# Grouping an attention pair's TensorE calls by array form, and queueing weight splits one tile later

## The chip, the cores and the metric

The kernel runs on one core of a Trainium2 chip. The metric is the device time of one execution in microseconds (us), from a few runs; the span of a profiled execution runs from the first to the last instruction. In the profile PE is TensorE's matmuls, PEld its weight loads, ACT ScalarE, DVE VectorE, POOL GpSimd, and SP the queue that issues the DMAs.

## The reference

Three blocks follow each other. Tokens are 1792 (4 batches of 448), the model width is 768, 12 heads of 64.

```python
scores = scale * np.matmul(q, k.transpose(0, 1, 3, 2)) - np.log(S)
attn = 1.0 / (1.0 + np.exp(-scores))
x = np.matmul(attn, v)                      # heads side by side: 1792 x 768
rms = np.sqrt(np.mean(x * x, axis=-1, keepdims=True) + 1e-06)
xn = x / rms * rms_g
g = xn @ w_gate; val = xn @ w_val           # 768 -> 1536
x = g * sigmoid(g) * val @ w_out            # 1536 -> 768
a = x @ w1; b = x @ w2                      # 768 -> 1024
out = (a * b @ w3) @ w_out2                 # 1024 -> 1024 -> 768
```

q, k and v are float32, and the weights arrive as float64. w3 and w_out2 can be multiplied with each other first; the kernel does that.

## The kernel before, in words

Everything is unrolled, and a list scheduler in the framework fixes the order of the instructions on each engine from the order in which the code issues them; tile pools set which buffer must come free before an instruction may write. Each engine works its own list strictly in turn.

**Weights.** A weight tile (128 rows of 768 or 512 columns) is loaded as pairs of 32-bit words into a `wd` buffer (two of these, `load_double`, L86), turned into float32 by `to_float` (L89 to L110: one Abs on ACT, L94, then four DVE operations, L95, L96, L104, L107, into a `wf` buffer, of which there are two), and split into a high and a low fp32r part by `split_weight`: a copy on ACT (L113) and a subtraction on POOL (L114). The results are `ws` tiles, of which there are four; `o` tiles are the same for w_out2. `Weights.split_to` (L174) does decode and split of a tile in one go. Every product of weights and activations then takes three matmuls (L230 to L232, or L266 to L268 for w3 by w_out2) of 128 x 128 on 448 or 384 columns.

**Attention.** A pair of heads is one step, 24 pairs in all. `load_pair` brings q, k and v of the pair into one `raw` tile. `scores(p, c)` multiplies key block c with q into a PSUM tile `sc` (two of these) and ACT takes the sigmoid into an `a` tile (L304). Blocks 0 to 2 use the array as two halves of 64 rows, one head in each (L300); block 3 holds the last 64 keys of both heads and uses the whole array (L303). `attend(p, c)` multiplies v with `a` into the PSUM tile `av` (one of these): blocks 0 to 2 as two halves of 64 columns (L317), block 3 on the whole array (L319). So there are three forms of the array: 64 x 128, 128 x 64 and 128 x 128, and the weight products use the last. After block 3 the result goes out: ACT copies it (L322), squares it (L327, L330), POOL adds the squares (L331), and a DMA writes it to memory (L324).

**Stages.** The first is the loop over `i` (L543): pairs 0 to 11, the eight decodes of w_out2 (`decode_wo2`, two in each of the first four passes), and, from i = 5 on, 16 groups of w3 by w_out2 (`w3o_group`, 24 matmuls each, two in a pass). It ends with `rms_norm(1)`; x tiles of batch 0 (`split_x`, L357 load, L358, L245, L246) are made in its last six passes. The second stage (about 200 to 650 us) is a list of units (`first_units`): accumulations of 18 or 36 matmuls for the gate, value, out, w1 and w2 products of batches 0 and 1. Between the units the steps of the other 12 pairs are dealt out evenly, six to a pair:

```python
yield lambda: scores(p, 0)
yield lambda: scores(p, 1)
yield lambda: (attend(p, 0), scores(p, 2))
yield lambda: (attend(p, 1), scores(p, 3))
yield lambda: attend(p, 2)
yield lambda: (attend(p, 3), load_pair(p + 2))
```

`run` (L527) loads ahead, runs a unit, and splits the next weight tile. The third stage (650 us on) has no attention: Winograd products of batches 2 and 3.

## Time and profile before

| | |
|---|---|
| runs | 1145.35, 1145.58, 1146.7 us, median 1145.58 us |
| profiled execution | 1145.92 us, span 1144.2 us |
| PE busy | 1112.4 us, 97% of the span |
| DVE, ACT, POOL busy | 632.3, 474.4 and 373.6 us |
| mean granted TensorE clock | 0.994 of full speed |

In the rows further down, a line of the timeline gives start, length, engine, line of the code, operation, tile written and read, shapes, how many records it merges (a call in one of the half forms leaves four records, a whole-array call of attention two), and in brackets how long the engine stood idle before and what it waited for. A PE length contains pipeline time, so the step from one start to the next is the better measure. The table by stage gives for each stretch the busy time of every engine, the granted clock (1.00 is 2.4 GHz, half is 1.2 GHz), the DMA engines' share and GB/s.

### The profile page before, as it was taken

To read this page: it belongs to the slowest core of one execution; us is meant where nothing else is said; L and a number is where in the kernel's file an instruction comes from. 1 tells how busy PE (TensorE), PEld (TensorE's weight loads), DVE (VectorE), ACT (ScalarE), POOL (GpSimd) and SP (SyncE) were. 2 spreads that over 40 slices of the span, in tenths; PEclk is the share of its full clock that TensorE was granted. 3 is DMA by queue.
4 is the path that set the end of the run, shared out by engine and by line. 5 is a ranking of instruction groups with operands and counts; after the bars stand their busy time and mean duration, and the time that the engine had idled before them with its cause. 6 is when DMAs were issued, how large, how long until landed. Compare 5 with 4: busy or idle time off the path is not lost.

```text
span 1144.2 us, 13902 instructions
## 1 busy us (share of the span) xinstructions
PE 1112.4 (97%) x5204; PEld 898.4 (79%) x5204; DVE 632.3 (55%) x873; ACT 474.4 (41%) x768; POOL 373.6 (33%) x276
## 2 busy tenths in 40 slices
PE   7689998999999999999999999999999999999998
PEld 2256767778777877877777799999989999899997
DVE  4765347764546554543544255598998222777600
ACT  6655554444434433433443334444444232433321
POOL 2431223122222312121222222466666222566420
PEclk9989998999999999999999999999999999999999
DMA  6655556553535354444443225221112210111131
GB/s 245 225 162 174 186 183 228 173 198 120 173 111 200 117 178 140 165 147 147 166 142 142 68 79 163 100 74 56 56 56 71 69 56 19 56 58 54 37 100 52
DMA packets 54930, 141.41 MB, mean 124 GB/s; under 512 B 5200, under 2 KB 28752, under 8 KB 54864
## 3 DMA queue, kind: packets, MB, share of 16 engines
q1 hardware_dynamic: 54864, 140.53, 36.6%
q8 instruction: 41, 0.67, 0.2%
q14 instruction: 25, 0.20, 0.1%
HBM read 105.91 MB, written 34.60 MB: 123 GB/s over the span
## 4 chain that ended last, share of the span: by engine, by line
PE 80%; DVE 2%; DMA 1%; POOL 0%; ACT 0%; issue 0%; SPq 0%; POOLq 0%; ACTq 0%
PE psm L230 18%; PE psm L231 17%; PE psm L232 17%; PE w L230 7%; PE w L231 7%; PE w L232 7%; PE sc L300 3%; PE av L317 3%; PE sc L303 1%; PE av L319 1%; DMA xs<-x 1%; POOL ws L114 0%; DVE s L438 0%; DVE wd L147 0%; DVE s L145 0%
## 5 line engine op out<-in xcount | busy, mean ns | idle before, releaser
L114 POOL TENSOR_TENSOR ws<-wf,ws 128x768 fp32r<-128x768 f32 (+1 forms) x104 | 175.5, 1687 | 546.8 <-ACT ws L113 546.8
L230 PE MATMUL w<-w,ws 128*128 128x448 f32 x420 | 154.4, 368 | 2.0 <-ACT w L245 1.5
L231 PE MATMUL w<-w,ws 128*128 128x448 f32 x420 | 154.3, 367 | 0.0
L232 PE MATMUL w<-w,ws 128*128 128x448 f32 x420 | 154.0, 367 | 0.0
L94 ACT ACTIVATE mag<-wd 128x768 f32<-128x768 f32 (+1 forms) x76 | 65.4, 860 | 158.3 <-DVE wf L96 60.0
L96 DVE TENSOR_SCALAR wf<-mag 128x768 uint32<-128x768 uint32 (+1 forms) x76 | 44.0, 580 | 139.8 <-POOL ws L114 138.1
L230 PE MATMUL psm<-x,ws 128*128 128x448 f32 x288 | 112.5, 391 | 1.7 <-ACT x L245 1.7
L231 PE MATMUL psm<-x,ws 128*128 128x448 f32 x288 | 106.7, 370 | 3.0 <-DVE x L246 3.0
L113 ACT ACTIVATE ws<-wf 128x768 fp32r<-128x768 f32 (+1 forms) x104 | 78.9, 759 | 72.6 <-PE psm L232 39.8
L114 POOL TENSOR_TENSOR ws<-wd,ws 128x384 fp32r<-128x384 f32 x80 | 87.7, 1112 | 61.1 <-ACT ws L113 61.1
L230 PE MATMUL psm<-hm,ws 128*128 128x448 f32 x288 | 107.4, 373 | 0.0
L232 PE MATMUL psm<-x,ws 128*128 128x448 f32 x288 | 106.2, 369 | 0.0
L231 PE MATMUL psm<-hm,ws 128*128 128x448 f32 x288 | 105.7, 367 | 0.0
L232 PE MATMUL psm<-hm,ws 128*128 128x448 f32 x288 | 104.9, 364 | 0.0
L304 ACT ACTIVATE a<-sc,bias_s 128x896 f32<-128x896 f32 x96 | 86.1, 907 | 25.3 <-PE sc L300 16.7
L114 POOL TENSOR_TENSOR ws<-s,ws 128x384 fp32r<-128x384 f32 x60 | 71.8, 1200 | 63.2 <-ACT ws L113 56.1
L95 DVE TENSOR_SCALAR mag<-mag 128x768 f32<-128x768 f32 (+1 forms) x76 | 43.8, 577 | 83.6 <-ACT mag L94 83.3
L107 DVE SCALAR_TENSOR_TENSOR wf<-wd,wf 128x768 uint32<-128x768 uint32 (+1 forms) x76 | 87.1, 1146 | 1.4
L230 PEld LDWEIGHTS w<-w,ws 128*128 128x128 f32 x420 | 78.7, 188 | 11.1 <-ACT w L245 1.8
L300 PE MATMUL sc<-raw 64*128 64x448 f32 x288 | 74.1, 596 | 11.1 <-ACT a L304 5.7
L232 PEld LDWEIGHTS w<-w,ws 128*128 128x128 f32 x420 | 78.9, 188 | 7.4
L231 PEld LDWEIGHTS w<-w,ws 128*128 128x128 f32 x420 | 78.8, 188 | 7.2
(117 smaller groups left out, 2161.0 us busy)
## 6 DMA issues: line engine op xcount, KB each, us to landing
raw<-in_qkv SPq DMA_DIRECT2D x24, 736.0 KB, 6.1
wd<-in_wo SPq DMA_DIRECT2D x20, 768.0 KB, 4.9
wd<-in_w SPq DMA_DIRECT2D x16, 768.0 KB, 4.9
wd<-in_wg SPq DMA_DIRECT2D x12, 768.0 KB, 4.7
wd<-in_wv SPq DMA_DIRECT2D x12, 768.0 KB, 4.9
wd<-in_w SPq DMA_DIRECT2D x16, 512.0 KB, 4.1
w<-wf SPq DMA_DIRECT2D x16, 384.0 KB, 2.5
wf<-w3o SPq DMA_DIRECT2D x24, 256.0 KB, 2.8
```

The lines of the kernel that those rows point to most:

```text
L94: nc.scalar.activation(mag, hi.bitcast(F32), AF.Abs)
L95: nc.vector.tensor_scalar(out=mag, in0=mag, scalar1=HI_MIN, scalar2=HI_MAX, op0=ALU.max, op1=ALU.min)
L96: nc.vector.tensor_scalar(out=u, in0=mag.bitcast(U32), scalar1=3, scalar2=0x3FFFFFFF, op0=ALU.logical_shift_left, op1=ALU.bitwise_and,)
L107: nc.vector.scalar_tensor_tensor(out=u, in0=lo, scalar=29, in1=u, op0=ALU.logical_shift_right, op1=ALU.bitwise_or)
L113: nc.scalar.activation(t[:, 0, :w], f[:, :w], AF.Copy)
L114: nc.gpsimd.tensor_tensor(out=t[:, 1, :w], in0=f[:, :w], in1=t[:, 0, :w], op=ALU.subtract)
L230: nc.tensor.matmul(ps, wl, xt[:, 0, :], start=first, stop=False)
L231: nc.tensor.matmul(ps, wh, xt[:, 1, :], start=False, stop=False)
L232: nc.tensor.matmul(ps, wh, xt[:, 0, :], start=False, stop=last)
L300: nc.tensor.matmul(ps[:, j, :S], r[d, k], r[d, Q0 : Q0 + S], start=True, stop=True)
L304: nc.scalar.activation(a, ps[:, :, :S], AF.Sigmoid, bias=bias_s, scale=1.0 / math.sqrt(D))
L317: nc.tensor.matmul(ps[d, :], r[:, v + j * D : v + (j + 1) * D], a[:, j, :], start=(c == 0), stop=False)
```

## The change

Five edits. `attend` takes a list of blocks and begins the accumulation with block 3; what it did after the last block is now `take_out`. In the loop over `i`, a pair's attend calls run one pass later, all four in one row once the w3o groups run (i = 5 on), else as (3, 0) and (1, 2) between the score calls. In the second stage a pair is two steps, `first_half` (all of the pair before, then scores 0 and 1) and `second_half` (scores 2 and 3). `split_to` and `decode_wo2` now decode a tile first and then split the tile decoded before it (`late`, `finish`); `get` splits the tile at once if that has not happened. The first pair's `raw` tile is loaded by three DMAs, of 576, 384 and 512 columns, instead of one of 1472.

```diff
--- before.py
+++ after.py
@@ -120,6 +120,7 @@
 
         def __init__(self):
             self.seq, self.raw, self.split = [], {}, {}
+            self.late = None
             self.n_load = self.n_split = self.out = 0
             self.loaded, self.blocks = [], self.winograd_blocks()
 
@@ -171,30 +172,44 @@
                 self.raw[self.n_load] = t
                 self.n_load += 1
 
-        def split_to(self, n):
+        def split_to(self, n, flush=False):
+
             n = min(n, len(self.seq) - 1)
             while self.n_split <= n and len(self.split) < self.BUFS:
                 i = self.n_split
                 self.load_to(i)
                 src, kt, double, keep = self.seq[i]
                 f = self.raw.pop(i)
+                w = WT if kt is None else kt * P
+                if double:
+                    f = to_float(f, w)
+                    if keep is not None:
+                        nc.sync.dma_start(out=keep, in_=f[:, :w].rearrange("p (k c) -> p k c", c=P))
+                    self.out -= 1
+                self.finish()
                 t = wp.tile([P, 2, WT], F32R, tag="ws", bufs=self.BUFS, name="ws")
+                self.split[i] = [t, 2]
+                self.n_split += 1
                 if kt is None:
                     for j in range(2):
                         split_weight(t[:, :, j * WH : (j + 1) * WH], next(self.blocks), WH)
+                elif double:
+                    self.late = (i, t, f, w)
                 else:
-                    w = kt * P
-                    if double:
-                        f = to_float(f, w)
-                        if keep is not None:
-                            nc.sync.dma_start(out=keep, in_=f[:, :w].rearrange("p (k c) -> p k c", c=P))
                     split_weight(t, f, w)
                     self.out -= 1
-                self.split[i] = [t, 2]
-                self.n_split += 1
+            if flush:
+                self.finish()
+
+        def finish(self):
+            if self.late:
+                split_weight(*self.late[1:])
+                self.late = None
 
         def get(self, i):
             self.split_to(i)
+            if self.late and self.late[0] == i:
+                self.finish()
             t = self.split[i]
             t[1] -= 1
             if not t[1]:
@@ -250,8 +265,9 @@
 
     def decode_wo2(j):
         f = to_float(raw2.pop(j), DM)
+        W.finish()
         t = wo2p.tile([P, 2, DM], F32R, tag=f"o{j}", name=f"o{j}")
-        split_weight(t, f, DM)
+        W.late = (None, t, f, DM)
         o2.append(t)
 
     NH = DM // 2
@@ -286,7 +302,10 @@
     def load_pair(p):
         if p < NP:
             t = raw[p] = at([P, RAWW], F32, "raw")
-            nc.sync.dma_start(out=t, in_=qkv[p // HP, p % HP])
+
+            cuts = (0, S + P, V0, RAWW) if p == 0 else (0, RAWW)
+            for c, d in zip(cuts, cuts[1:]):
+                nc.sync.dma_start(out=t[:, c:d], in_=qkv[p // HP, p % HP][:, c:d])
 
     def scores(p, c):
 
@@ -303,23 +322,24 @@
             nc.tensor.matmul(ps[:, 0, :S], r[:, k], r[:, Q0 : Q0 + S], start=True, stop=True)
         nc.scalar.activation(a, ps[:, :, :S], AF.Sigmoid, bias=bias_s, scale=1.0 / math.sqrt(D))
 
-    def attend(p, c):
-
-        r, a = raw[p], probs.pop((p, c))
-        b, h = divmod(p, HP)
-        if c == 0:
-            av[p] = ps_av.tile([P, 512], F32, tag="av", bufs=1, name="av")[:, :S]
-        ps = av[p]
-        v = V0 + c * P
-        if c < 3:
+    def attend(p, cs):
+
+        r = raw[p]
+        for c in cs:
+            a, v = probs.pop((p, c)), V0 + c * P
+            if c == 3:
+                av[p] = ps_av.tile([P, 512], F32, tag="av", bufs=1, name="av")[:, :S]
+                nc.tensor.matmul(av[p], r[:, v : v + P], a[:, 0, :], start=True, stop=False)
+                continue
             for j in range(2):
                 d = slice(j * D, (j + 1) * D)
-                nc.tensor.matmul(ps[d, :], r[:, v + j * D : v + (j + 1) * D], a[:, j, :], start=(c == 0), stop=False)
-            return
-        nc.tensor.matmul(ps, r[:, v : v + P], a[:, 0, :], start=False, stop=True)
-        raw.pop(p), av.pop(p)
+                nc.tensor.matmul(av[p][d, :], r[:, v + j * D : v + (j + 1) * D], a[:, j, :], start=False, stop=(c == 2))
+
+    def take_out(p):
+        b, h = divmod(p, HP)
+        raw.pop(p)
         x = at([P, S], F32, "xr")
-        nc.scalar.activation(x, ps, AF.Copy)
+        nc.scalar.activation(x, av.pop(p), AF.Copy)
         d = xd[b, h] = dram.tile([P, S], F32, name=f"x{b}_{h}")
         nc.sync.dma_start(out=d, in_=x)
         if h == 0:
@@ -541,28 +561,32 @@
     raw2[0] = load_double(wo2[0], KD)
     raw2[1] = load_double(wo2[1], KD)
     for i in range(NA + 1):
+        beside = i > KF2 // 2
+        if beside:
+            attend(i - 1, (3, 0, 1, 2))
         if i < NA:
             scores(i, 0)
             scores(i, 1)
-        if i:
-            attend(i - 1, 2)
-            attend(i - 1, 3)
-            if i + 2 < NA:
-                load_pair(i + 2)
-        if i > KF2 // 2:
-            w3o_group(*groups.pop(0))
-        if i < NA:
-            attend(i, 0)
-            scores(i, 2)
-            attend(i, 1)
-            scores(i, 3)
-        if i > KF2 // 2 and len(groups) > 1:
+        if i and not beside:
+            attend(i - 1, (3, 0))
+        if beside:
             w3o_group(*groups.pop(0))
         for j in (2 * i, 2 * i + 1):
             if j < KF2:
                 decode_wo2(j)
             if j + 2 < KF2:
                 raw2[j + 2] = load_double(wo2[j + 2], KD)
+        if i < NA:
+            scores(i, 2)
+            scores(i, 3)
+        if i and not beside:
+            attend(i - 1, (1, 2))
+        if i:
+            take_out(i - 1)
+            if i + 2 < NA:
+                load_pair(i + 2)
+        if beside and len(groups) > 1:
+            w3o_group(*groups.pop(0))
         if 2 * i + 2 >= KF2:
             W.split_to(2 * KF2 - len(groups) + 3)
         if i == HP:
@@ -580,20 +604,25 @@
     pools["h"] = pool("h", "right")
 
 
-    def pair_steps(p):
-        yield lambda: scores(p, 0)
-        yield lambda: scores(p, 1)
-        yield lambda: (attend(p, 0), scores(p, 2))
-        yield lambda: (attend(p, 1), scores(p, 3))
-        yield lambda: attend(p, 2)
-        yield lambda: (attend(p, 3), load_pair(p + 2))
+    def first_half(p):
+        if p > NA:
+            attend(p - 1, (3, 0, 1, 2))
+            take_out(p - 1)
+            load_pair(p + 1)
+        if p < NP:
+            scores(p, 0)
+            scores(p, 1)
+
+    def second_half(p):
+        scores(p, 2)
+        scores(p, 3)
 
     steps = [lambda: (load_pair(NA), load_pair(NA + 1))]
     for p in range(NA, NP):
-        steps += list(pair_steps(p))
+        steps += [lambda p=p: first_half(p), lambda p=p: second_half(p)]
         if p % HP == 0 and p > NA:
-            steps.insert(-1, lambda b=p // HP - 1: rms_norm(b))
-    steps += [lambda: None, lambda: None, lambda: rms_norm(B - 1)]
+            steps.append(lambda b=p // HP - 1: rms_norm(b))
+    steps += [lambda: first_half(NP), lambda: None, lambda: rms_norm(B - 1)]
     early = [lambda k=k: split_x(1, k) for k in range(KD)]
     units = list(first_units())
     first = [units[j] for j in (0, 1, 4, 2, 3, 5)] + units[6:]
```

On PE the change moves attention calls. This is the pass i = 7 of the first stage (S calls are L300 and L303 before, L319 and L322 now; A calls L317 and L319 before, L332 and L336 now; `x4` are two calls of two heads, `x2` one); before, the pass has them in two bundles, among the w3o groups' matmuls:

```order
L268 MATMUL psm<-o_377,ws 128x384
L337 MATMUL psm<-acc,ones 128x448
L300 MATMUL sc<-raw 128x448 x4
L317 MATMUL av<-a,raw 64x448 x2
L319 MATMUL av<-a,raw 128x448
L266 MATMUL psm<-o_188,ws 128x384
...
L317 MATMUL av<-a,raw 64x448 x2
L300 MATMUL sc<-raw 128x448 x2
L317 MATMUL av<-a,raw 64x448 x2
L303 MATMUL sc<-raw 128x448
L266 MATMUL psm<-o_188,ws 128x384
```

Now:

```order
L357 MATMUL psm<-acc,ones 128x448
L332 MATMUL av<-a,raw 128x448
L336 MATMUL av<-a,raw 64x448 x6
L319 MATMUL sc<-raw 128x448 x4
L282 MATMUL psm<-o_176,ws 128x384
...
L284 MATMUL psm<-o_352,ws 128x384
L319 MATMUL sc<-raw 128x448 x2
L322 MATMUL sc<-raw 128x448
L282 MATMUL psm<-o_176,ws 128x384
```

The array's form changed seven times in a pass before, and changes five times now.

On ACT the change moves the copies of the decode (L113) against the Abs (L94). This is where w_out2's tiles 5 and 6 (`o_319`, `o_367`) are split, around the pass i = 3; before:

```order
L94 ACTIVATE mag<-wd 128x768
L304 ACTIVATE a<-sc,bias_s 128x896
L113 ACTIVATE o_319<-wf 128x768
L304 ACTIVATE a<-sc,bias_s 128x448
L304 ACTIVATE a<-sc,bias_s 128x896
L113 ACTIVATE o_367<-wf 128x768
L304 ACTIVATE a<-sc,bias_s 128x896
L94 ACTIVATE mag<-wd 128x768
L322 ACTIVATE xr<-av 128x448
L330 ACTIVATE sq<-xr 128x448
```

Now (tiles 5 and 6 are `o_294` and `o_342`):

```order
L94 ACTIVATE mag<-wd 128x768
L113 ACTIVATE o_294<-wf 128x768
L323 ACTIVATE a<-sc,bias_s 128x896 x2
L94 ACTIVATE mag<-wd 128x768
L113 ACTIVATE o_342<-wf 128x768
L323 ACTIVATE a<-sc,bias_s 128x448
L342 ACTIVATE xr<-av 128x448
L350 ACTIVATE sq<-xr 128x448
```

The Abs of the next tile now stands ahead of the copy of the tile before it.

On SP, at the end of the first stage, the load of the last x tile of batch 0 (`xs`, from pair 5's `x_5`) stands behind other DMAs; before:

```order
L190 DMA wg_94<-wf 128x768
L324 DMA x_5_1320<-xr 128x448
L86 DMA wd<-in_wg 128x1536
L271 DMA w3o<-w3ot 128x384
L357 DMA xs<-x_5_595 128x448
```

Now:

```order
L187 DMA wg_94<-wf 128x768
L86 DMA wd<-in_wg 128x1536
L344 DMA x_5_1348<-xr 128x448
L187 DMA wv_95<-wf 128x768
L86 DMA wd<-in_wv 128x1536
L287 DMA w3o<-w3ot 128x384
L377 DMA xs<-x_5_632 128x448
```

The write of the next decoded tile (`wv_95`) and the next weight load have moved ahead of it.

## Rows read from the trace of the kernel before

**Rows 1.** The table by stage: stretch, length, busy PE PEld DVE ACT POOL, clock, DMA.
```profile
0.00:60.00 60.00, 42.58 (x148) 12.57 (x148) 36.02 (x39) 37.94 (x51) 20.09 (x16) 1.00 0.66 230
60.00:74.00 14.00, 10.63 (x36) 6.71 (x36) 8.12 (x12) 5.21 (x10) 4.32 (x3) 0.76 0.57 181
74.00:180.00 106.00, 105.34 (x514) 72.74 (x513) 51.74 (x75) 59.69 (x91) 28.12 (x21) 1.00 0.52 169
180.00:200.00 20.00, 15.32 (x66) 13.44 (x64) 16.09 (x23) 9.17 (x13) 3.64 (x2) 0.83 0.83 293
200.00:650.00 450.00, 450.00 (x2072) 347.99 (x2071) 235.47 (x316) 182.18 (x257) 103.42 (x57) 1.00 0.44 151
```

**Rows 2.** Timeline of PE, the first w3o group.
```profile
60.02 0.44 PE L266 MATMUL psm<-o,ws 128*128 128x384 f32 x1 [1.04 <-POOL ws L114]
60.30 0.34 PE L267 MATMUL psm<-o,ws 128*128 128x384 f32 x1
60.47 0.34 PE L268 MATMUL psm<-o,ws 128*128 128x384 f32 x1
...
66.61 0.69 PE L266 MATMUL psm<-o,ws 128*128 128x384 f32 x1 [3.35 <-POOL ws L114]
```

**Rows 3.** Timelines, end of the first stage: of ACT, POOL, DVE, and of PE.
```profile
172.62 0.85 ACT L113 ACTIVATE ws<-wf 128x768 fp32r<-128x768 f32 x1 [1.52 <-PE psm L268]
...
178.10 1.57 POOL L331 TENSOR_TENSOR acc<-acc,sq 128x448 f32<-128x448 f32 x1 [0.26 <-ACT sq L330]
...
183.48 0.95 DVE L107 SCALAR_TENSOR_TENSOR wf<-wd,wf 128x768 uint32<-128x768 uint32 x1
...
193.76 0.74 PE L231 MATMUL psm<-x,ws 128*128 128x448 f32 x1 [3.00 <-DVE x L246]
```

**Rows 4.** Timeline of PE, one score call between weight products, second stage.
```profile
237.39 0.36 PE L232 MATMUL psm<-x,ws 128*128 128x448 f32 x1
237.68 1.02 PE L300 MATMUL sc<-raw 64*128 64x448 f32 x4
...
238.94 0.37 PE L231 MATMUL psm<-x,ws 128*128 128x448 f32 x1
239.15 0.37 PE L232 MATMUL psm<-x,ws 128*128 128x448 f32 x1
```

**Rows 5.** Timelines of PE and of its weight loads, two attend calls in a row.
```profile
28.56 1.72 PE L317 MATMUL av<-a,raw 128*64 128x448 f32 x8 [1.21 <-ACT xr L322]
30.22 1.02 PE L303 MATMUL sc<-raw 128*128 128x448 f32 x2
...
28.99 0.14 PEld L317 LDWEIGHTS av<-a,raw 128*64 128x64 f32 x2 [0.23 <-issue]
```

**Rows 6.** Timeline of ACT, decode of w_out2's tiles 5 to 7.
```profile
38.44 0.88 ACT L94 ACTIVATE mag<-wd 128x768 f32<-128x768 f32 x1
...
47.78 0.84 ACT L113 ACTIVATE o<-wf 128x768 fp32r<-128x768 f32 x1 [1.68 <-DVE wf L107]
48.53 0.99 ACT L304 ACTIVATE a<-sc,bias_s 128x896 f32<-128x896 f32 x1
49.42 0.88 ACT L94 ACTIVATE mag<-wd 128x768 f32<-128x768 f32 x1
```

**Rows 7.** The page, DMA issues: KB each, median us from issue to landing.
```profile
wd<-in_wo SPq DMA_DIRECT2D x20, 768.0 KB, 4.9
```

**Rows 8.** Timelines of DVE and of POOL, decode of the same tiles.
```profile
43.73 0.55 DVE L96 TENSOR_SCALAR wf<-mag 128x768 uint32<-128x768 uint32 x1
44.31 0.96 DVE L104 SCALAR_TENSOR_TENSOR wf<-wd,wf 128x768 uint32<-128x768 uint32 x1
45.30 2.45 DVE L107 SCALAR_TENSOR_TENSOR wf<-wd,wf 128x768 uint32<-128x768 uint32 x1
...
44.76 2.18 POOL L114 TENSOR_TENSOR o<-wf,o 128x768 fp32r<-128x768 f32 x1 [3.10 <-ACT o L113]
```

**Rows 9.** Timeline of SP, the load of the last x tile of batch 0.
```profile
182.99 0.38 SPq L357 DMA_DIRECT2D xs<-x  x1
```

## Prediction

> **What bounds the kernel now.** The table by stage tells where time can be won [rows 1]. From 74 to 180 us and from 200 to 650 us PE is busy 105.34 of 106 and 450 of 450 us, and no other engine much over half: there only shorter PE work counts. In the first 60 us PE is busy 42.58 us, in the next 14 us 10.63, and from 180 to 200 us 15.32: there it waits. In the last two of these the mean granted clock is 0.76 and 0.83, that is, for 2 x 0.24 x 14 = 6.7 us and 2 x 0.17 x 20 = 6.8 us the chip gave 1.2 instead of 2.4 GHz, both times in or after an idle stretch of PE. Then I read on the timeline whom PE waits for: POOL's subtraction for the first w3o group [rows 2], and the last x tile of batch 0 [rows 3].
>
> **What a change of the array's form costs.** No row states it, so I take it from two places. Around a score call between weight products, from the product before it (237.39) to the second one after it (238.94) are 1.55 us, two steps of products of 0.205 (238.94 to 239.15) among them: call + 2 changes = 1.14 us [rows 4]. Two attend calls in a row, then a call of another form: 30.22 - 28.56 = 1.66 us = 2 calls + 1 change [rows 5]. Together a call takes 0.73 us and a change 0.20. The gap ahead of the call alone, 0.29 against 0.205 [rows 4], is the low end, 0.09 us. I take 0.19, near the upper end: the two equations hold the whole price where PE has no idle time.
>
> **Part 1, grouping in the second stage.** Counted in PE's lists, the form changes 130 times there before and 67 times now: 63 x 0.19 = 12.0 us off a stage in which PE never waits. Against it, the four matmuls of pair 12's first two score calls no longer stand side by side, one for each head, but one by one among the products of a unit, so two calls of 0.73 take twice as long: 1.5 us. **10.5 us** remain. For this the sigmoids must stay hidden: in the new list at least 36 products (36 x 0.205 = 7 us) stand between a pair's score calls and the calls that need their results, and a sigmoid takes 0.99 us [rows 6].
>
> **Part 2, grouping in the first stage.** After the first w3o group has its weights, 48 changes become 32: 16 x 0.19 = **3.0 us**, as PE is full there, too [rows 1].
>
> **Part 3, the decode of the weights (up to 67 us).** Two tiles go round in 11.0 us: the Abs of tile 5 starts at 38.44, that of tile 7 at 49.42 [rows 6]. The last of this is a queue: the copy of tile 6 waits 1.68 us for DVE, a sigmoid of 0.99 follows, and the Abs of tile 7 stands behind both. In the new order the Abs stands ahead of that copy. What then limits the round is one `wd` buffer: its load, 4.9 us [rows 7], the Abs, 0.9, and DVE. DVE's four operations are two like L96 and two like L104, 2 x 0.55 + 2 x 0.96 = 3.0 us, and one took 2.45 us while a POOL subtraction ran beside it [rows 8]; with that 4.5. The sum is 10.3 us, 0.7 less, and over four rounds about 3 us. So I expect the first w3o group at 57 instead of 60.02 and its second half at 62.7 instead of 66.61 [rows 2]. PE also has more to do meanwhile: two score calls (1.5 us) and nine products of the next group (9 x 0.17 = 1.5) now stand ahead of that second half, and one matmul of an attend call (0.7) no longer: 2.3 us. 3.9 + 2.3 = **6.2 us**. Bounds: 0, if the loads set the pace after all, and 8, if the round shrinks by twice as much.
>
> **Part 4, the clock.** It falls between 60 and 74 us for 6.7 us, which PE fills with work from 66.61 on: about half of it, **3.4 us**, is lost [rows 1, 2]. The fall lies in the wait of 3.35 us; with that nearly filled I expect none. Low end 0.
>
> **Part 5, the end of the first stage.** I count from the ACT copy at 172.62, which PE's half w3o group releases and behind which DVE's decodes follow. The x tile's load goes out at 182.99, 10.4 us later [rows 9], and PE runs at 193.76, 21.1 us later [rows 3]. Now the load stands behind the write of the next decoded tile, which waits for the DVE operation that ended at 184.43, 11.8 us after the copy; less about 1, since the POOL addition of 1.57 us moves behind it and no longer stretches DVE [rows 3]; plus three issues of some 0.4: the load goes out 12.1 us after the copy. From there on 10.8 us passed before; I add 0.6, because the weight load now goes out closer ahead of it. PE runs 23.5 us after the copy: 2.4 us lost. But of pair 11's attend calls two (2 x 0.73 = 1.5 us), done before that copy until now, fall into this wait. Net **-1.0 us**; from -4, if the queue of SP is later than I think, to +2.4, if the clock, which falls here too, stays up. Here PE also gets a new wait, for the sum of squares (the copy out of `av` now follows all four calls); it lies ahead of the x tile's wait and is covered by it.
>
> **Part 6, at nothing.** The first pair's rows in three parts let PE start sooner; that is hidden, since the decodes, not the pairs, set the first group. If ACT comes late to the first Abs, it costs at most a sigmoid or two, 1 to 2 us. Splits one tile late in the second stage: in ACT's new list each copy stands at least 58 products (58 x 0.205 = 12 us) ahead of its first use, counted from the last PE result that stands before it in the list. The third stage keeps its order.
>
> **Sum.** 10.5 + 3.0 + 6.2 + 3.4 - 1.0 = 22.1 us. The profiled span less this is 1144.2 - 22.1 = 1122.1; around the span lie 1145.92 - 1144.2 = 1.7 us, so 1123.8, and the median of the runs is 0.3 below the profiled execution: **1123.5 us**. Its own range by the bounds: 1114 to 1130.
>
> **Rivals.**
> - *The loads set the start.* Parts 3 and 4 give nothing: 1123.5 + 9.6 = 1133. For it: DMA engines 66% busy at 230 GB/s [rows 1]. Against it: the ACT idle time in the round ends with DVE, not with a load [rows 6]. Chance 0.15.
> - *A change of form costs only the gap ahead of the call.* Part 1 gives 63 x 0.09 - 1.5 = 4.2, part 2 gives 1.4: 1123.5 + 7.9 = 1131. Against it: both equations above. Chance 0.07.
> - *Weight loads come into the open between calls of one form.* A load takes 0.14 us [rows 5]. If it could not run beside the matmul before it, some 96 new neighbours of one form in the second stage (four to a pair, two loads each) would cost 96 x 0.14 = 13 us: 1137. Against it: the two attend calls in a row leave no room for it, and the load at 28.99 runs under the matmuls that PE shows from 28.56 on [rows 5]. The Trainium skill ("TensorE: Matmul & The Clock Gate", Part 3) has a weight load overlap a running matmul only where the row group differs, which attend calls of 128 rows never offer; the trace does not bear that out here. Chance 0.05.
> - *Slower: the late split comes due at its use.* `get` splits a tile at once if nobody has. If in the second stage ACT's copy took its place only when the unit comes up, PE would wait for a copy and a subtraction, 0.84 + 2.18 = 3.0 us [rows 6, 8], for each of the 52 decoded tiles: 156 us, 1123.5 + 156 = 1280. The case decides from 8 tiles on (22.1 / 3.0 = 7.4). For it: the split is issued in the code right ahead of the unit. Against it: the 58 products of part 6, and ACT busy only 182 of 450 us [rows 1]. Chance 0.05.
> - That the change doesn't do what it says is no case: the lists of the engines show it.
>
> **How the numbers follow.** The forecast has 0.68. The range of 1114 to 1136 takes in the first two rivals and leaves out the slower one, the 1137 and the tails. A difference of 0.2% (2.3 us) is about what a measurement of this kernel can tell from no change. All cases but the slower one are faster by more than that; for a failure that I do not see I add 0.03 to the same and 0.02 to slower: faster 0.90, same 0.03, slower 0.07.
>
> **What would show it.** Right: stage two shorter by 10 us with PE still never idle; the second half of the first w3o group at 61 to 64 us, and a granted clock of 1.00 from there to the end of the first stage; the wait for the last x tile still there. Wrong: in the second stage PE idle after an attend or a score call, or waiting for POOL or ACT before a unit; a first group that starts at 60 as before.

## The result, and the profile after

The changed kernel takes 1133.85 us (median of 4 runs, 1133.39 to 1134.88) against 1145.46 of the kernel before (4 runs): ratio 0.9901, 95% interval 0.9884 to 0.9918, 11.3 us less by the ratio (11.6 between the medians). The forecast was 1123.5 us, so the sign and the range held, but only about half of the forecast gain of 22 us came. The profiled execution has a span of 1131.6 us (1144.2 before): 12.6 us to account for.

The table by stage of the changed kernel, the same stretches and columns as [rows 1]:

```profile
0.00:60.00 60.00, 42.90 (x148) 13.04 (x148) 39.20 (x39) 37.41 (x48) 21.60 (x15) 0.94 0.67 226
60.00:74.00 14.00, 11.34 (x50) 9.74 (x51) 7.24 (x14) 8.10 (x14) 4.37 (x4) 0.88 0.57 193
74.00:180.00 106.00, 101.41 (x502) 70.50 (x500) 54.02 (x80) 57.64 (x90) 27.41 (x21) 1.00 0.56 177
180.00:200.00 20.00, 16.80 (x76) 14.91 (x77) 12.76 (x18) 9.35 (x14) 4.79 (x3) 0.91 0.76 265
200.00:650.00 450.00, 450.00 (x2116) 362.18 (x2115) 243.94 (x317) 184.41 (x264) 105.05 (x60) 1.00 0.44 152
```

In the second stage PE is full as before. What is new stands in the third line: between 74 and 180 us PE was busy 105.34 of 106 us [rows 1], and now 101.41. So 3.9 us of waits have come where there was hardly any. The first stage, whose changes the forecast put at 11.6 us (parts 2 to 5), ends only 0.26 us sooner: its end is taken here as the moment at which the last x tile of batch 0 reaches PE, the first units of the second stage having begun shortly before. The timeline of PE answers to [rows 2] and to the last line of [rows 3]:

```profile
62.20 0.69 PE L282 MATMUL psm<-o,ws 128*128 128x384 f32 x1 [5.31 <-POOL ws L114]
69.91 0.44 PE L282 MATMUL psm<-o,ws 128*128 128x384 f32 x1 [0.46 <-POOL ws L114]
92.87 1.02 PE L332 MATMUL av<-a,raw 128*128 128x448 f32 x2 [1.93 <-ACT a L323]
104.07 1.02 PE L319 MATMUL sc<-raw 64*128 64x448 f32 x4 [1.69 <-ACT a L323]
181.71 1.86 PE L357 MATMUL psm<-acc,ones 128*128 128x448 f32 x2 [2.65 <-POOL acc L351]
193.50 0.47 PE L246 MATMUL psm<-x,ws 128*128 128x448 f32 x1 [1.50 <-DVE x L261]
```

The first w3o group starts at 62.20, neither at the forecast 57 nor at the 60.02 of before; its second half at 69.91. Two waits for sigmoids are new, at 92.87 and 104.07, and so is one for the sum of squares. The last x tile reaches PE at 193.50 (193.76 before).

**Why the start did not get shorter.** The timelines of DVE, POOL, SP and ACT in the changed kernel, one turn of a `wd` buffer (tiles are counted from 0; tile 5 is loaded, decoded, and replaced by tile 7):

```profile
40.68 2.45 DVE L104 SCALAR_TENSOR_TENSOR wf<-wd,wf 128x768 uint32<-128x768 uint32 x1
43.16 1.77 DVE L107 SCALAR_TENSOR_TENSOR wf<-wd,wf 128x768 uint32<-128x768 uint32 x1
...
40.20 2.12 POOL L114 TENSOR_TENSOR o<-wf,o 128x768 fp32r<-128x768 f32 x1 [3.71 <-ACT o L113]
42.28 1.84 POOL L351 TENSOR_TENSOR acc<-acc,sq 128x448 f32<-128x448 f32 x1
...
33.55 0.33 SPq L86 DMA_DIRECT2D wd<-in_wo  x1
45.00 0.33 SPq L86 DMA_DIRECT2D wd<-in_wo  x1
...
38.50 0.89 ACT L94 ACTIVATE mag<-wd 128x768 f32<-128x768 f32 x1 [2.35 <-DMA wd<-in_wo]
49.88 0.90 ACT L94 ACTIVATE mag<-wd 128x768 f32<-128x768 f32 x1 [2.27 <-DMA wd<-in_wo]
```

The load of tile 5 goes out at 33.55. The Abs follows 4.95 us later, and the next load into the same buffer goes out at 45.00, as soon as DVE's L107 has read the buffer (43.16 + 1.77 = 44.93): 11.45 us a turn, two tiles. That is the turn that part 3 described, load, Abs and DVE's four operations, but DVE's share is 45.00 - 38.50 - 0.89 = 5.6 us and not 4.5. Both two-input operations, L104 and L107, run into one on POOL: one into the late subtraction of the tile before, the other into the addition of the squares (so in tiles 3, 5 and 7; in tiles 4 and 6 only L104 does).

**Where the waits in the middle come from.** The timelines of PE and of ACT in the changed kernel:

```profile
85.01 1.02 PE L322 MATMUL sc<-raw 128*128 128x448 f32 x2
...
90.73 0.66 ACT L94 ACTIVATE mag<-wd 128x512 f32<-128x512 f32 x1 [3.02 <-DMA wd<-in_w]
91.30 1.52 ACT L323 ACTIVATE a<-sc,bias_s 128x896 f32<-128x896 f32 x2
...
101.02 0.67 ACT L94 ACTIVATE mag<-wd 128x512 f32<-128x512 f32 x1 [1.27 <-DMA wd<-in_w]
```

In these rows ACT takes its list in turn. Each time it stands at an Abs whose tile has not landed, the sigmoids queue behind it (the second time behind a table load, too, until 103.01), and behind them PE. But it stood there in the kernel before as well, and PE did not wait; timelines of ACT and PE before:

```profile
92.56 0.66 ACT L94 ACTIVATE mag<-wd 128x512 f32<-128x512 f32 x1 [3.68 <-DMA wd<-in_w]
93.13 1.51 ACT L304 ACTIVATE a<-sc,bias_s 128x896 f32<-128x896 f32 x2
...
89.88 1.02 PE L303 MATMUL sc<-raw 128*128 128x448 f32 x2
...
97.47 0.97 PE L317 MATMUL av<-a,raw 128*64 128x448 f32 x4
```

From a pair's last score call to the attend calls that need its sigmoid PE had 7.6 us of other work (89.88 to 97.47, two score calls of the next pair in it), and the sigmoids were done 4.8 us after that call (93.13 + 1.51 = 94.64). Now the attend calls stand ahead of the next pair's scores, PE is there after 5.9 us (85.01 to 90.94, where its wait of 1.93 begins), and the sigmoids are done after 7.8 us (92.82).

**The end of the first stage.** The timelines of SP and DVE there:

```profile
180.64 0.32 SPq L187 DMA_DIRECT2D wv<-wf  x1
181.01 0.42 SPq L86 DMA_DIRECT2D wd<-in_wv  x1
182.01 0.50 SPq L377 DMA_DIRECT2D xs<-x  x1
...
189.03 0.68 DVE L378 SCALAR_TENSOR_TENSOR xs<-xs,g_sb,r 128x448 f32<-128x448 f32 x1 [3.68 <-DMA xs<-x]
189.63 2.95 DVE L363 RECIPROCAL r<-t 128x448 f32<-128x448 f32 x1
192.50 0.94 DVE L261 TENSOR_TENSOR x<-xs,x 128x448 fp32r<-128x448 f32 x1
```

The load of the last x tile stands behind the write of a decoded tile, as part 5 said, and on DVE its subtraction comes behind a reciprocal of 2.95 us, as it did before (2.94 us from 189.54).

**The second stage.** One meeting of attend and score calls among the products, on the timeline of PE in the changed kernel:

```profile
236.64 0.36 PE L247 MATMUL psm<-x,ws 128*128 128x448 f32 x1
236.84 0.91 PE L332 MATMUL av<-a,raw 128*128 128x448 f32 x2
237.69 2.48 PE L336 MATMUL av<-a,raw 128*64 128x448 f32 x12
240.09 1.77 PE L319 MATMUL sc<-raw 64*128 64x448 f32 x8
241.80 0.47 PE L245 MATMUL psm<-x,ws 128*128 128x448 f32 x1
242.10 0.37 PE L246 MATMUL psm<-x,ws 128*128 128x448 f32 x1
```

From the product at 236.64 to the second one after the calls, at 242.10, are 5.46 us. The second and third of the three attend calls in one line start at 238.49 and 239.24, so a call among its like takes 0.75 us. Less two steps of 0.205 and six calls of 0.75 this leaves 0.55 us for three changes of form, 0.18 each: the prediction took 0.19. Nothing new shows between calls of one form.

### The profile page after: what moved, and what is told of

It is laid out like the page before. It is cut to its first block, busy times and chain, and to the rows that moved or that the text cites. A ratio compares the mean times of both kernels' runs of the same rounds, so it can differ in the third digit from the quotient of the medians.

```text
span 1131.6 us, 13919 instructions
## 1 busy us (share of the span) xinstructions
PE 1098.9 (97%) x5204; PEld 904.4 (80%) x5204; DVE 640.6 (57%) x873; ACT 472.3 (42%) x768; POOL 372.7 (33%) x276
## 4 chain that ended last, share of the span: by engine, by line
PE 81%; DVE 1%; DMA 1%; issue 0%; ACT 0%; POOL 0%; SPq 0%; POOLq 0%; ACTq 0%
PE psm L245 17%; PE psm L246 17%; PE psm L247 17%; PE w L245 7%; PE w L246 7%; PE w L247 7%; PE sc L319 3%; PE av L336 3%; PE sc L322 1%; PE av L332 1%; DMA xs<-x 1%; POOL ws L114 0%; DVE w L261 0%; PE psm L357 0%; DVE x L261 0%
## 5 line engine op out<-in xcount | busy, mean ns | idle before, releaser
L94 ACT ACTIVATE mag<-wd 128x768 f32<-128x768 f32 (+1 forms) x76 | 65.6, 863 | 163.2 <-DVE wf L96 67.9
L96 DVE TENSOR_SCALAR wf<-mag 128x768 uint32<-128x768 uint32 (+1 forms) x76 | 43.7, 575 | 135.9 <-POOL ws L114 134.1
L113 ACT ACTIVATE ws<-wf 128x768 fp32r<-128x768 f32 (+1 forms) x104 | 78.9, 758 | 73.1 <-PE psm L247 43.7
L245 PE MATMUL psm<-x,ws 128*128 128x448 f32 x288 | 108.1, 377 | 0.0
L246 PE MATMUL psm<-x,ws 128*128 128x448 f32 x288 | 105.8, 367 | 1.5 <-DVE x L261 1.5
L247 PE MATMUL psm<-x,ws 128*128 128x448 f32 x288 | 105.1, 366 | 0.0
L323 ACT ACTIVATE a<-sc,bias_s 128x896 f32<-128x896 f32 x96 | 83.4, 907 | 10.4 <-PE sc L319 10.2
L107 DVE SCALAR_TENSOR_TENSOR wf<-wd,wf 128x768 uint32<-128x768 uint32 (+1 forms) x76 | 87.0, 1145 | 1.3
L95 DVE TENSOR_SCALAR mag<-mag 128x768 f32<-128x768 f32 (+1 forms) x76 | 43.5, 572 | 74.7 <-ACT mag L94 74.1
L104 DVE SCALAR_TENSOR_TENSOR wf<-wd,wf 128x768 uint32<-128x768 uint32 (+1 forms) x76 | 83.5, 1098 | 2.6
```

The source lines that it names most:

```text
L94: nc.scalar.activation(mag, hi.bitcast(F32), AF.Abs)
L95: nc.vector.tensor_scalar(out=mag, in0=mag, scalar1=HI_MIN, scalar2=HI_MAX, op0=ALU.max, op1=ALU.min)
L96: nc.vector.tensor_scalar(out=u, in0=mag.bitcast(U32), scalar1=3, scalar2=0x3FFFFFFF, op0=ALU.logical_shift_left, op1=ALU.bitwise_and,)
L104: nc.vector.scalar_tensor_tensor(out=u, in0=hi, scalar=0xC0000000, in1=u, op0=ALU.bitwise_and, op1=ALU.bitwise_or)
L107: nc.vector.scalar_tensor_tensor(out=u, in0=lo, scalar=29, in1=u, op0=ALU.logical_shift_right, op1=ALU.bitwise_or)
L113: nc.scalar.activation(t[:, 0, :w], f[:, :w], AF.Copy)
```

## Theories and experiments

**Theory A**: the gain is the changes of form saved in the second stage. The first stage is set by the turn of a `wd` buffer with DVE's stretched operations in it, by Abs operations that stand ahead of sigmoids, and by its end; late splits and first rows in parts give nothing or cost a little there. **Theory B**, in several shapes: the three parts need one another, or the DMA engines (0.66 busy) are the limit whatever the order. All ratios are to the kernel before, with 95% intervals.

### Second stage alone

```diff
 # first stage as in the kernel before: one call at a time (attend_one),
 # splits at once, one DMA; only the second stage uses attend(p, (3, 0, 1, 2))
+            attend(p - 1, (3, 0, 1, 2))
+            take_out(p - 1)
```

> The kernel before with its first stage as it was (calls in the old order, splits at once, one DMA for the first pair); only the second stage's pairs of heads go to TensorE in two pieces. Theory A (the gain of the change is the changes of form in the second stage, 63 at 0.15 to 0.19 us, plus a clock fall that moved): rows up to 193.8 us as in the kernel before, then 9.5 us less between there and 640, so 1145.5 - 9.5 = 1136, between 1134.5 and 1137. Theory B (the rest of the change carries part of it: the second stage is only as fast as its weights, which the late splits keep ahead): a gain of 5 us or less, 1140 or more.

Measured: 1135.2 us, 0.9908 (0.9893 to 0.9923). Timeline of PE, then a line of the table by stage:

```profile
60.27 0.44 PE L281 MATMUL psm<-o,ws 128*128 128x384 f32 x1 [1.04 <-POOL ws L114]
67.41 0.69 PE L281 MATMUL psm<-o,ws 128*128 128x384 f32 x1 [3.88 <-POOL ws L114]
```
```profile
200.00:650.00 450.00, 450.00 (x2123) 363.32 (x2122) 242.38 (x318) 183.26 (x263) 104.82 (x60) 1.00 0.44 152
```

The first stage is that of before (the clock between 180 and 200 us is 0.83, too), and the span falls from 1144.2 to 1134.0, by 10.2 us (10.7 between the medians, 1145.86 and 1135.2). Part 1 forecast 10.5. The whole change is faster than this by 1.4 us between the medians, which the intervals cannot tell from nothing. So nearly all of the gain is part 1, and all else in the change is worth about 1.4 us, not 11.6.

### The change without its parts in turn

```diff
 # one load
-            cuts = (0, S + P, V0, RAWW) if p == 0 else (0, RAWW)
+            cuts = (0, RAWW)
 # split at once (in split_to, and the same in decode_wo2)
-                elif double:
-                    self.late = (i, t, f, w)
```

> The change with the first pair loaded by one DMA again; all else as changed. Theory A (the parts gave the first score call 1 us and cost the first weight tile 2.6): first score call back at 5.4 us, first Abs of a wo2 tile at about 11 us instead of 13.52, so the first w3o group, which the decode decides, starts 2 us earlier, at about 60, and the whole takes some 1132, 2 us less than the change (1133.9). Theory B (the start of the decode sets nothing, because what the first tile gains the later tiles wait for again, at a DMA or at VectorE): group at 62 as in the change, time the same within 1 us. Theory C (the parts are needed: the sooner first pair is what lets the chip's clock rise sooner and ScalarE be free sooner): time 1 to 3 us above the change.

> The change with every weight tile split right after its own conversion again (calls of a form together and the first pair in three parts stay). Theory A (the late split gave the start nothing, since it puts the subtraction on POOL beside VectorE's two-input operations of every next tile and stretches a round of two tiles from 11.0 to 11.4 us; it also puts Abs operations that wait for a DMA ahead of the sigmoids in the middle of the first stage, two TensorE waits of 4.5 us together): L104 falls back to 0.96 us in every second tile, first w3o group at 60 to 62, the waits at 90.4 and 102.0 are gone, time 1130 to 1134. Theory B (late splits are what keeps the grouped order from waiting for ScalarE): first w3o group after 64, time 1136 to 1140.

> Both stages with the calls of one form together, but splits at once and the first pair by one DMA: the change without its other two parts. Theory A: the second stage's 9.5 us and the first stage's 3.0 come with the order of the calls alone, and the start is no worse than in the change: 1130 to 1134, at or under the change. Theory B (the three parts need one another): 1136 or more.

Measured, with the change itself for the fourth corner:

| | first pair in three parts | first pair by one DMA |
|---|---|---|
| splits one tile late | 0.9901 (0.9884 to 0.9918) | 0.9884 (0.9867 to 0.9901), 1131.33 us |
| splits at once | 0.9910 (0.9892 to 0.9928), 1135.22 us | 0.9893 (0.9877 to 0.9908), 1133.24 us |

No two neighbours are apart by their intervals. Both rows put the cost of the parts at 0.0017 (1.9 us), both columns the gain of the late split at 0.0009 (1.0 us). Calls in groups alone already give what the change gives; they are 2.0 us faster between the medians than the run with the second stage alone (1133.24 against 1135.2), which the intervals cannot tell from nothing either. With splits at once (and the parts) three expectations of Theory A fell, and its time, 1130 to 1134, was missed by 1.2 us. The first group is not sooner (63.39; 60.92 without the parts). DVE's operations are not faster: L104 still takes 1.8 to 1.9 us on average in both runs with splits at once. And the waits for sigmoids are not gone: PE waits 1.3 us up to 87.67 and 1.0 up to 103.85, and 0.4 and 1.6 us in the run without the parts. So they are not the late splits' alone. L104 and L107 together take 3.34 us a tile in the change and 2.87 with one DMA, 2.78 and 2.87 with splits at once, 2.79 before: the stretch of both operations belongs to the late splits and the parts together, not to the late splits alone. And with one DMA the first Abs is 2.0 us sooner, at 11.49 instead of 13.52, but the first group only 1.0 us, at 61.17; between the timelines of ACT and DVE in that run lies the rest:

```profile
46.23 0.92 ACT L94 ACTIVATE mag<-wd 128x768 f32<-128x768 f32 x1 [0.25 <-DMA wd<-in_wo]
53.89 0.65 ACT L94 ACTIVATE mag<-wd 128x512 f32<-128x512 f32 x1
...
54.58 1.58 DVE L95 TENSOR_SCALAR mag<-mag 128x512 f32<-128x512 f32 x1 [1.47 <-ACT mag L94]
56.26 1.41 DVE L96 TENSOR_SCALAR wf<-mag 128x512 uint32<-128x512 uint32 x1
59.04 0.42 DVE L95 TENSOR_SCALAR mag<-mag 128x512 f32<-128x512 f32 x1
```

The last wo2 tile is 3.65 us ahead of the change's (46.23 against 49.88), the first w3 tile not at all (53.89 against 53.88): these two lie in different buffers, and the tile ahead of the w3 tile in its buffer, tile 6, comes no sooner here (43.15 against 42.57). Between tiles 1 and 7, in the other buffer, a turn takes 10.85 us in this run (13.68 to 46.23) and 11.4 in the change.

### What sets the turn of the buffer

```diff
 # subtraction of the eight wo2 tiles on VectorE (n_sub counts the splits; its lines are left out)
-        nc.gpsimd.tensor_tensor(out=t[:, 1, :w], in0=f[:, :w], in1=t[:, 0, :w], op=ALU.subtract)
+        eng = nc.vector if n_sub[0] <= KF2 else nc.gpsimd
+        eng.tensor_tensor(out=t[:, 1, :w], in0=f[:, :w], in1=t[:, 0, :w], op=ALU.subtract)
 # third buffer, first stage only (the loads one tile further ahead are left out)
+        if n <= 24 and n % 3 == 0:
+            t = att["pool"].tile([P, WT, 2], U32, tag="wd3", bufs=1, name="wd3")
```

> The change with the subtraction of the eight wo2 tiles on VectorE instead of POOL. Theory A (the decode at the start is VectorE's time plus a load in turn, and VectorE's two-input operations take 2.45 instead of 0.96 us beside POOL's subtraction): L104 at 0.96 us for all eight, VectorE 3.0 us a tile up to the point where the buffer is free, a round of two tiles 9 to 10 instead of 11.4 us in spite of the eight more operations of about 1.1 us, first w3o group at 55 to 59 instead of 62.20, time 1128 to 1132. Theory B (loads set the round): L104 faster, but the round stays at 11 us or more, VectorE idles longer, group at 61 or later, time 1133 or more.

> The change with a third wd buffer for the 24 weight tiles of the first stage. Theory A (the start goes at the pace of one wd buffer, whose cycle is load 4.95 + Abs 0.95 + VectorE 5.4 = 11.4 us for two tiles, and the two TensorE waits at 90.4 and 102.0, 4.5 us together, are ScalarE standing at an Abs that waits for such a load): with three buffers the load leaves the cycle, the start falls to VectorE's 2 x 5.4 = 10.8 us a round, so the first w3o group at about 60 instead of 62.20, both later waits gone, time 1128 to 1130. Theory B (VectorE and the DMA engines are full, the buffer is no limit): group at 62 or later, time within 1 us of the change, 1133 to 1135.

Subtraction on VectorE (DVE): 1126.09 us, 0.9837 (0.9823 to 0.9852). Timelines of DVE and PE:

```profile
33.74 0.95 DVE L118 TENSOR_TENSOR o<-wf,o 128x768 fp32r<-128x768 f32 x1
34.60 0.95 DVE L104 SCALAR_TENSOR_TENSOR wf<-wd,wf 128x768 uint32<-128x768 uint32 x1
...
57.41 0.44 PE L286 MATMUL psm<-o,ws 128*128 128x384 f32 x1 [1.77 <-POOL ws L118]
```

VectorE does one operation of 0.95 us more for each tile and is faster by it, since L104 takes 0.95 us for all eight tiles (2.08 on average in the change). Tile 5 to tile 7 is 10.0 us (Abs at 37.42 and 47.40) instead of 11.4, and the first group starts at 57.41, where the forecast had it for the change itself. Theory A holds, and the loads are no limit: the DMA share of the first 60 us is 0.74 here against 0.67.

Third buffer: 1128.73 us, 0.9861 (0.9846 to 0.9876). The turn falls to 10.0 us as well (Abs of tiles 5 and 7 at 32.64 and 42.62), although L104 still takes 2.26 us on average. Between 58 and 173 us PE has no wait left over 0.5 us, and the last x tile reaches it at 188.08. The first group does not start sooner, though, at 62.98: that expectation was wrong. Waits of PE between 20 and 63 us say why:

```profile
PE sc L325 <- ACT a L329: 5.7, 4, 2.2
PE av L338 <- ACT xr L348: 3.1, 2, 2.6
PE sc L328 <- ACT a L329: 3.1, 2, 2.0
```

The weights are there in time, and now PE is late with the attention calls ahead of them, because ACT, which does the Abs operations sooner, comes later to sigmoids and copies (11.9 us of waits for ACT, 8.0 in the change); the granted clock of the first 60 us is lower, too, 0.89 against 0.94, and what each of the two costs was not taken apart. What the buffer gave lies behind the group's start: from there to the last x tile are 125.1 us instead of 131.3.

### The same in the kernel before, and with more tiles

The edit of the first run above, made in the kernel before; then in the change for all 24 tiles of the first stage (`n_sub[0] <= 3 * KF2`).

> The kernel before with the wo2 subtractions on VectorE, nothing else. Theory A (the cycle of a wd buffer with VectorE in it set the start before the change too, where every second tile had its operations stretched to 2.45 us): L104 at 0.96 us in all, first w3o group at 56 to 58 instead of 60.02, second half at 61 to 64 instead of 66.61, 1140 to 1143 instead of 1145.5. Theory B (before the change, the queue on ScalarE, a copy that waits for VectorE and a sigmoid ahead of the Abs, sets the round of 11.0 us, as the prediction had it): first group at 59.5 to 60.5, time within 1.5 us of before.

> The change with the subtractions of all 24 weight tiles of the first stage on VectorE (the run with the eight wo2 tiles there took 1126.1). Theory A (after the start PE is the bound of the first stage and the remaining tiles' subtractions are hidden wherever they are): within 1.5 us of 1126.1. Theory B (VectorE's stretched operations also set the waits for ScalarE and the end of the stage): 1122 to 1124. Theory C (16 more operations of 0.65 to 1 us on VectorE, 37 of 68 us busy already, come ahead of the conversions that free the wd buffers): 1128 or more.

In the kernel before: 1137.34 us, 0.9928 (0.9915 to 0.9941), 8.2 us less by the ratio; timeline of PE:

```profile
56.15 0.45 PE L270 MATMUL psm<-o,ws 128*128 128x384 f32 x1 [0.79 <-POOL ws L118]
61.90 0.45 PE L270 MATMUL psm<-o,ws 128*128 128x384 f32 x1 [1.53 <-POOL ws L118]
```

More than Theory A expected, and against the reading of [rows 6] that a queue on ACT was the last limit of the round: with POOL off the wo2 tiles the start gains 3.9 us at the first half and 4.7 at the second. The 8.2 us and the change's 11.3 add up to 19.5, the run with both has 18.7: within the intervals the two gains add up. With all 24 tiles on VectorE: 1125.12 us, 0.9823 (0.9809 to 0.9837), no different from eight; behind the start it does not matter where the subtraction runs.

### The end of the first stage

```diff
 # x tiles of batch 0 early
-        if i > HP and i - HP <= KD:
-            split_x(0, i - HP - 1)
+        if HP < i <= HP + 3:
+            split_x(0, 2 * (i - HP) - 2)
+            split_x(0, 2 * (i - HP) - 1)
 # and, in the second run (with one DMA too): sum of squares late
-    rms_norm(1)
     w3o_group(*groups.pop(0))
+    rms_norm(1)
```

> The change with the six x tiles of batch 0 made two at a time right after the sum of squares of batch 0 (three steps of the first stage instead of six), so that none is left for its end. Theory A (PE's last wait before the second stage, 1.86 us up to 193.50, is the load of the last x tile, behind the write of a decoded tile on SP's queue): that wait is gone, the second stage starts at 191 to 192, time 1131 to 1133; the wait of 2.65 us for the sum of squares stays. Theory B (what is won there comes back as waits for ScalarE or VectorE between 100 and 150 us, where the x tiles now are made): time 1134 or more.

> The change with the first pair by one DMA, the x tiles of batch 0 made early, and the sum of squares of batch 1 behind the last half w3o group instead of ahead of it. Theory A (the end of the first stage is two waits, for the sum of squares and for the last x tile, in which the saved changes of form are lost): both waits are gone (2.8 and 2.6 us in the kernel with one DMA, which took 1131.3), second stage starts at about 187 to 188.5 instead of 192.4, time 1126 to 1128. Theory B (PE only waits elsewhere, for the weights of the first units or for batch 1's x tiles): second stage or its first units wait as long, time 1130 to 1132.

With the x tiles early: 1131.97 us, 0.9889 (0.9872 to 0.9905), as Theory A had it; the wait at the second stage's first units is gone, but 1.9 us less is within the interval. With the sum late as well: 1132.23 us, 0.9890 (0.9875 to 0.9904), where 1126 to 1128 was expected. Timeline of PE, and one line of the chain that ended there (start, us, what):

```profile
198.50 0.68 PE L245 MATMUL psm<-x,ws 128*128 128x448 f32 x1 [3.44 <-ACT x L260]
```
```profile
190.00 2.86 DVE r L363
```

Both waits are gone, and one of 3.44 us has come in their place: the x tiles of batch 1 need the reciprocal, which starts at 190.00 here and at 187.28 in the run before, where the sum stood ahead. Theory B was right here: the wait for the sum was paid early for something that is needed soon after.

### Put together

> The change with both: the wo2 subtractions on VectorE and a third wd buffer in the first stage (alone they took 1126.1 and 1128.7, the change 1133.9). Theory A (both cut the same cycle of a wd buffer, load plus Abs plus VectorE, at the start, 4 to 5 us each; only the third buffer also removes the waits for ScalarE's Abs at 83 to 107 us, 3.1 us in the run with VectorE alone): not the sum of 7.8 and 5.1, but 1126.1 less about 3, 1122 to 1125, with the first w3o group at 54 to 57. Theory B (independent gains): 1119 to 1122.

> As the run with the wo2 subtractions on VectorE and the third buffer, and the first pair by one DMA and the x tiles of batch 0 two at a time. Theory A (one DMA lets the first tile land 2 us sooner and the start is a chain of tiles; the early x tiles remove the wait of 2.6 us for the last of them): 3 to 4 us under the run without these two, 1119 to 1122. Theory B (the first tile's 2 us are lost again in the chain, and ScalarE and VectorE pay for the early x tiles in the middle): within 1.5 us of the run without them.

Subtraction on VectorE and the third buffer: 1124.72 us (five runs, 1119.75 to 1125.5), 0.9805 (0.9785 to 0.9824): not the sum of both, as Theory A expected of two cuts of the same turn. With one DMA and the early x tiles: 1118.14 us, 0.9760 (0.9746 to 0.9774), 6.6 us less between the medians and 5.2 by the ratios, where 3 to 4 were expected; by the intervals it can be 2 to 8. Lines of its table by stage, and of its timeline of PE:

```profile
60.00:74.00 14.00, 14.00 (x73) 10.31 (x72) 8.45 (x15) 8.18 (x14) 4.00 (x3) 1.00 0.75 234
74.00:180.00 106.00, 103.63 (x508) 75.72 (x507) 50.71 (x73) 60.62 (x89) 27.62 (x20) 0.98 0.55 186
```
```profile
167.67 1.02 PE L367 MATMUL psm<-acc,ones 128*128 128x448 f32 x2 [2.37 <-POOL acc L361]
```

PE has no wait left between 60 and 74 us, and the clock is 1.00 there, as part 4 had it for a filled wait. Of the waits behind, that for the sum of squares remains. This version beats both kernels: 27.5 us (2.4%) off the kernel before, 15.7 off the change by the medians.

## Why the prediction was right or wrong

- **Part 1 was right**, mechanism and size: 10.5 us forecast; 10.2 by the spans and 10.7 by the medians where it stands alone. PE is full in the second stage. The rivals that would have taken it away (price only in the gap ahead of a call, weight loads in the open, late splits due at their use) are out.
- **Part 2** is not shown by itself. A change of form costs what was taken, but the two waits for sigmoids, 3.6 of the 3.9 us between 74 and 180 us, use up its 3.0; calls in groups alone, against the second stage alone, gave 2.0 us, within the intervals. "PE is full there, too" was read from the old order. For the second stage the forecast counted what stands between a score call and the calls that need its result; for the first it did not, and there ACT's loads make the sigmoids late.
- **Part 3 was the step that failed.** It named the right turn (load, Abs, DVE) and mis-sized one term: "with that 4.5. The sum is 10.3 us". DVE took 5.6 and the turn 11.45 us, since not one but both of its two-input operations run beside POOL. The run with the subtraction on VectorE took POOL's subtraction away alone: 10.0 us a turn, group at 57.41, 7.8 us faster. Three more things were wrong.
  - The starting value of 11.0 was the shortest turn: from tile 1 to tile 7 it is 11.8 on average before (14.10 to 49.42) and 11.4 now (15.64 to 49.88), so it did shrink, by 0.4 and not 0.7.
  - The first half of the group does not hang on this buffer but on the other one, from tile 0 to the first w3 tile, whose four turns take 10.3 on average before (10.93 to 52.26) and 10.1 now (13.52 to 53.88).
  - Part 6 put the first rows in parts at nothing; their DMAs stand ahead of the first weights on SP's queue (issued at 3.54 instead of 2.59), and the first Abs came 2.6 us later, at 13.52 instead of 10.93, 2.0 of them by the run with one DMA; the table of four puts the whole cost at 1.9, within the intervals.

  In place of +6.2 the second half started 3.3 us later with 2.3 us more work ahead of it: -1.0.
- **Part 4** depended on part 3. The wait that it wanted filled is still there (5.31 us at 62.20), and the clock falls in it: 0.88 over the 14 us (0.76 before). Over the first 60 us it is 0.94, where it was 1.00 before.
- **Part 5** was right in mechanism and size: the x tile's load goes out 12.2 us after the ACT copy (169.84 to 182.01; 12.1 forecast), and PE runs 23.65 us after it (193.50; 23.5 forecast). The copy comes 2.8 us sooner than before, and 2.5 of them are lost up to 193.50, where 2.4 were forecast. The wait for the sum of squares, 2.65 us, lies ahead of that for the x tile, which still ends last: covered, as forecast. Where the x wait is taken away, it is what remains.
- **The rival "the loads set the start"** gave 1133, the measured time, but for another cause; that is luck. The DMA engines carry more where the turn is shorter (share 0.74 and 0.80 in the first 60 us with VectorE alone and with all four edits, against 0.67); the buffer, held by DVE, made the loads wait. And the measured time lies in the range because that takes in the rivals: the sum's own range, 1114 to 1130, misses it.

From the last x tile's product on the change gains 12.3 us, 10.2 of it by part 1 and 2 by the clock. Before, PE ran at a granted clock of 0.51 from 193.7 to 198.8 us, behind the wait for that tile; now the fall comes ahead of the wait, at 181.3 to 184.8 us (0.51), and the wait takes up what it costs. The forecast had this only as a bound of part 5.

What stays open: the two small parts of the change, late splits (about 1.0 us for) and first rows in parts (1.9 us against), are each within one interval; how much of the waits for sigmoids is the order of the calls and how much the lateness of the loads; and which of the last two edits, one DMA or the early x tiles, gives what the four have over the two.

## What to carry to other kernels

Price a change of the array's form from two equations over calls and changes, and count the changes in PE's list: where PE never waits, that sum is what is gained. Where a stage turns on a buffer, write down the turn with every operation at the length that it has beside its new neighbours, and ask which engine's neighbour the change moves there; moving a subtraction onto the busier engine won more than the reordering did in that stage. And where calls are regrouped, count in every stage what stands between a call and the one that needs its result, and what the engine between them may stand waiting for: ACT stood at its loads before the change, too, but only now did PE feel it.

## What the runs showed of the hardware that was not expected

In this kernel DVE's operations with two inputs do not share with POOL, they wait it out. In the changed kernel L104 at 40.68 ends at 43.13, 0.81 us after the subtraction on POOL (40.20 + 2.12 = 42.32); L107 at 43.16 ends at 44.93, 0.81 after the addition (42.28 + 1.84 = 44.12); alone each takes 0.96. Where DVE was first, POOL took longer: in [rows 8] L104 from 44.31 takes its 0.96, and the subtraction from 44.76 takes 2.18, alone 1.80. The Trainium skill ("SBUF — State Buffer", Who interferes with whom) says that a DVE instruction with two SBUF inputs contends with a GpSimd one that reads SBUF, and that the one that comes second stands until the other is done; by these rows the trace agrees.

Operations with one input were hit, too: in the run with one load, L95 on 512 columns took 1.58 us from 54.58 and L96 1.41 from 56.26, beside POOL's operations from 54.06 to 55.87 and from 56.25 to 57.39, and the same L95 0.42 at 59.04. And VectorE's own subtraction of 768 columns takes 0.95 us where POOL's takes 1.8 to 2.3, so that the engine with less to do was the dearer place for it.
